# The opening of a Fourier transform and feed-forward kernel: stores, w1 conversions and loads put into another order

## The chip, the cores and the metric

The kernel runs on one core of a Trainium2 chip. Five engines work side by side, each through its own list of instructions in order, and wait for each other by semaphores: TensorE (PE, matrix products; PEld is its weight load), VectorE (DVE), ScalarE (ACT), GpSimd (POOL) and SyncE (SP, which here issues only transfers). Sixteen DMA engines move data between the device memory and the on-chip memory; transfers are issued from SP, ACT or POOL. The metric is the device time of the whole kernel in microseconds (us), the median of several executions.

## The reference

For 8 batches of 3136 rows by 256 columns, the real part of a two-dimensional Fourier transform, then a feed-forward layer with a layer norm ahead of it and a residual around it:

```python
def _attn_ref(x):
    X = np.fft.fft(x, axis=1)
    X = np.fft.fft(X, axis=2)
    return X.real.astype(np.float32)

def _moe_ref(x, g_ln, w_ch1, w_ch2):
    mu = np.mean(x, axis=-1, keepdims=True)
    var = np.mean((x - mu) ** 2, axis=-1, keepdims=True)
    xn = (x - mu) / np.sqrt(var + 1e-06) * g_ln
    ch = np.maximum(xn @ w_ch1, 0.0) @ w_ch2
    return (x + ch).astype(np.float32)
```

`x` of the second function is the result of the first. `w_ch1` is 256 x 1024 and `w_ch2` is 1024 x 256; both come in as 64-bit floating-point numbers, which the kernel reads as 64-bit integers and converts to 32-bit numbers itself.

## The kernel before

**How the work is staged.** The transform along the 3136 rows is done in two steps. Step 1 takes a batch in 7 pieces (`load_x(b, i)`, 512 KB each, the last 256 KB): DVE folds a piece (`fold_zw`, L229 and L230; `fold_eo`, L235 and L236, folds further), PE multiplies it with a table (`step1`, L283 or L289 and L291), ACT copies the result to the tile `s1` (L301), and a transfer (`store1`, L305) writes it to `scratch` in the device memory. `ends` (POOL) and `step1_ends` (PE, then ACT L272) fill one column of `s1` that belongs to the pieces, so a store waits for them too. `relayout` (L312) reads `scratch` back in another order into `s2`; it waits until every store of the batch has landed, and until `clear_scratch` (L256) has put zeros into the rows that no piece fills. Step 2 (`step2(m, ...)`, L345) multiplies `s2` with the table `tab_s` and gives chunks of 256 tokens; "h" is ACT's rounded copy (`ckh`, L366), "l" is DVE's remainder (`ckl`, L370), "f" is ACT's full copy (`ck`, L368; `single`, L352).

**Tiles.** A tile s is one chunk of tokens by 128 of the 1024 hidden columns, 8 tiles to a chunk. `moe1_a(s)` is six products on PE into a PSUM tile `ab` (two buffers), then ACT's copy `asb` (L395), then DVE's two halves of `h` (L396, L397). `moe1_b(s)` is ACT's `h_hi` (L404) and DVE's `h_lo` (L405). `moe2(s)` is twelve products on PE (L440). From tile 6 on a loop runs `moe1_b(s-1)`, `moe1_a(s)`, `moe2(s-3)`, with all else hung into it by lists (`add`, `add_late`).

**Weights.** w1 and w2 come in four quarters each, 512 KB per quarter, into the four parts of one tile, `w1p_all` (`load_w1`, L587; `load_w2(n)`, L592, which overwrites w1's quarter n and so waits for its conversion). A conversion is `convert_m` (DVE, L558 and L560), `convert_z` (ACT, L567), `convert_b` (DVE, L572 and L573) and `finish_w1` (DVE, L601) or `finish_w2` (DVE, L633). For w1 a transform follows, in halves k of the 1024 columns: `transform_w1(k, i)` (PE, L611) takes quarter 2k+i, `round_w1(k)` (ACT, L619) makes the high part, `rest_w1(k)` (PE, L624) and `rest_w1_copy(k)` (ACT, L629) the low part. Tiles 0 to 3 need half k=0 only, tiles 4 to 7 half k=1. `split_w2` is a copy on ACT (L577) and a difference on POOL (L578).

**What sets the order.** On PE, ACT, DVE and POOL the program order is the order of execution for the whole kernel; for the opening, the lines before `main.append(True)`, this holds for SP as well. `warm_up(n, zeros)` is n products of zeros into a PSUM tile that nothing reads (L718).

Of the kernel before, what the change touches and what calls it, by code (L numbers as in the profile page):

```python
# [157 lines left out]
def tile_kernel(ctx: ExitStack, tc: tile.TileContext, x, w1, w2, tu, tab, tz, ty, tw, out):  # L158
# [35 lines left out]
    def load_x(b, i):  # L194
        n = 2 * len(held(i))
        in_order(nc.sync.dma_start(xs[:, i, :n], x[b, i, :, :n]))  # L196
# [22 lines left out]
    def fold_zw(b, i, eng):  # L219

        if i > 3 and b == 0:
            t = weights.tile([128, HW], F32, tag="h_hi", name=f"zw{b}_{i}", bufs=4)
        else:
            t = work.tile([128, 2 * 256], F32, tag="zw", name=f"zw{b}_{i}", bufs=3)
        n = len(held(i))
        z, w = (t[:, 256 * h:256 * h + 128 * n].rearrange("p (s d) -> p s d", s=n) for h in range(2))
        zw[b, i] = z, w
        a, c = xs[:, i, 0:n], xs[:, i, n:2 * n]
        eng.tensor_tensor(out=z, in0=a[:, :, 1:129], in1=c[:, :, 255:127:-1], op=ALU.add)  # L229
        eng.tensor_tensor(out=w, in0=a[:, :, 255:127:-1], in1=c[:, :, 1:129], op=ALU.add)  # L230
# [72 lines left out]
    def store1(b, i, eng=nc.sync):  # L303
        s = s1[b][:, 2 * i:2 * i + len(held(i))]
        in_order(eng.dma_start(scratch[b][2 * i:2 * i + len(held(i))].rearrange("s p d -> p s d"),  # L305
                               s.rearrange("p a h d -> p a (h d)")))
# [257 lines left out]
    def convert_z(key, wp):  # L564
        _, e = conv[key][:2] if key in conv else convert_e(key, wp)
        top = wp.bitcast(BF16).rearrange("p (n four) -> p n four", four=4)[:, :, 3]
        nc.scalar.activation(e, top, AF.Prelu, scale=2.0 ** -112, alpha=2.0 ** 32)  # L567
# [16 lines left out]
    def load_w1(n):  # L584
        wp = w1p_all[:, 4 * n:4 * n + 4].rearrange("p a d -> p (a d)").bitcast(I64)
        i, k = n % 2, n // 2
        nc.sync.dma_start(wp, w1[128 * i:128 * i + 128, 512 * k:512 * k + 512])  # L587
        w1p.append(wp)
# [38 lines left out]
    def rest_w1_copy(k):  # L627
        for j in range(2):
            nc.scalar.copy(w1_cols(w1_lo, k, j), psw.pop((k, j)))  # L629
# [91 lines left out]
    with tc.manual_schedule(engines={E.PE, E.Activation, E.DVE, E.Pool}):  # L721
        with tc.manual_schedule(engines={E.SP}):
            nc.vector.memset(one, 1.0)
            for t in (warm, warm_h):
                nc.vector.memset(t, 0.0)
            for n, t in ((2, warm), (1, warm_h)):
                warm_up(n, t)
            nc.scalar.dma_start(tu_s, tu)
            load_x(0, 0)
            nc.scalar.activation(one, one, AF.Sqrt)  # L730
            for i in range(1, 4):
                load_x(0, i)
            load_w1(0)
            for i in (4, 5, 6):
                load_x(0, i)
            load_w1(1)
            nc.sync.dma_start(tw_all, tw)
            nc.sync.dma_start(tz_s, tz)
            load_w1(2)
            load_w1(3)  # L740
            clear_scratch(0, nc.gpsimd, 0, 2)
            nc.gpsimd.memset(zmu, 0.0)
            nc.gpsimd.memset(masked, 0.0)
            ends(0, 0, 6)
            for i in range(3):
                fold_zw(0, i, nc.vector)
                step1(0, i)
            step1_ends(0, 0, 6)
            for i in range(3):
                store1(0, i, nc.gpsimd)  # L750
            fold_zw(0, 3, nc.vector)
            convert_z("w1_0", w1p[0])
            step1(0, 3)
            ends(0, 6, 10)
            ends(0, 10, NS)
            convert_m("w1_0", w1p[0])
            fold_zw(0, 4, nc.vector)
            convert_b("w1_0")
            nc.vector.tensor_scalar_mul(g_s, tu_s[:, 388:390], 2.0 ** -20)
            finish_w1(0)  # L760
            step1(0, 4)
            step1_ends(0, 6, 10)
            store1(0, 3, nc.gpsimd)
            store1(0, 4, nc.gpsimd)
            for i in (5, 6):
                fold_zw(0, i, nc.vector)
                fold_eo(0, i, nc.vector)
            step1(0, 5)
            convert_m("w1_1", w1p[1])
            step1_ends(0, 10, NS)  # L770
            store1(0, 5, nc.scalar)
            convert_z("w1_1", w1p[1])
            convert_b("w1_1")
            finish_w1(1)
            step1(0, 6)
            store1(0, 6, nc.scalar)
            nc.scalar.dma_start(tab_s[:, :, :gb[4]], tab[:, :, :gb[4]])
            load_w2(0, nc.scalar)
            convert_z("w1_2", w1p[2])
            nc.scalar.copy(minus, tw_all[:, 512:])  # L780
            convert_z("w1_3", w1p[3])
            convert_m("w1_2", w1p[2])
            convert_b("w1_2")
            finish_w1(2)
            convert_m("w1_3", w1p[3])
            relayout(0, 0, 2)
            relayout(0, 2, 4)
            load_w2(1)
            clear_scratch(0, nc.sync, 2, 8)
            load_w2(2)  # L790
            relayout(0, 4, 8)
            nc.sync.dma_start(tab_s[:, :, gb[4]:gb[8]], tab[:, :, gb[4]:gb[8]])
            relayout(0, 8, 16)
            transform_w1(0, 0)
            transform_w1(0, 1)
            round_w1(0)
            convert_b("w1_3")
            load_w2(3)
            nc.sync.dma_start(ty_s, ty)
            nc.sync.dma_start(tab_s[:, :, gb[8]:], tab[:, :, gb[8]:])  # L800
            for i in range(NU):
                load_x(1, i)
            clear_scratch(1, nc.sync)
            finish_w1(3)
            transform_w1(1, 0)
            rest_w1(0)
            convert_z("w2_0", w2p[0])
            rest_w1_copy(0)
            transform_w1(1, 1)
            round_w1(1)  # L810
            convert_m("w2_0", w2p[0])
            convert_b("w2_0")
            f0 = finish_w2(0)
            split(t1_hi, t1_lo, tu_s[:, 0:128])
            convert_z("w2_1", w2p[1])
            convert_m("w2_1", w2p[1])
            warm_up(2, warm_h)
            step2(0, "m")
            step2(0, "h")
            step2(0, "l")  # L820
            step2(1, "m")
            step2(1, "h", 0)
            step2(1, "l", 0)
            convert_b("w2_1")
            f = finish_w2(1)
            moe1_a(0, ((1, 0), (0, 0), (0, 1)))
            split_w2(0, f0)
            moe1_a(1, ((1, 0), (0, 0), (0, 1)))
            rest_w1(1)
            moe1_b(0)  # L830
            split_w2(1, f)
            moe1_a(2)
            moe1_b(1)
            moe1_a(3)
            moe1_b(2)
            rest_w1_copy(1)
            convert_z("w2_2", w2p[2])
            convert_m("w2_2", w2p[2])
            step2(0, "f")
            step2(1, "f")  # L840
            step2(1, "hl", 1)
            moe2(0)
            moe1_b(3)
            moe2(1)
            moe1_a(4)
            convert_b("w2_2")
            f = finish_w2(2)
            nc.gpsimd.tensor_scalar(out=neg, in0=ty_s[:, 1, 129:130], scalar1=2.0, scalar2=-1.0,
                                    op0=ALU.mult, op1=ALU.add)
            step2(2, "m")  # L850
            moe1_b(4)
            moe1_a(5)
            split_w2(2, f)
            step2(2, "hf")
            step2(2, "l")
            moe2(2)
            convert_z("w2_3", w2p[3])
            convert_m("w2_3", w2p[3])
            add_late(6, convert_b, "w2_3")
            add_late(6, lambda: w2f.append(finish_w2(3)))  # L860
            late[7].insert(0, (lambda: split_w2(3, w2f.pop()), ()))

        main.append(True)
        lag, last = 3, 8 * NCH
        for s in range(6, last):
            moe1_b(s - 1)
            moe1_a(s)
            for fn, args in late.get(s, ()):
                fn(*args)
            moe2(s - lag)  # L870
            for fn, args in after.get(s, ()):
                fn(*args)
        moe1_b(last - 1)
        inverse_std(LC)
        moe2(last - 3)
        for i, side in ((0, 0), (1, 0), (0, 1), (1, 1)):
            for t in (last - 2, last - 1):
                moe2(t, ((i, side),))
            finish_last(i, side)
# [19 lines left out]
```

## Time and profile before

| | us |
|---|---|
| median of 3 executions | 982.49 (982.42 to 983.33) |
| the profiled execution | 982.3 |
| its span, first to last instruction | 980.5 |
| so outside the span | 1.8 |

In the rows of the timeline the first number is the start in us from the span's start, the second the time to the end of the last instruction of the row, and the bracket tells how long the engine had been idle and who released it. In the chain of waits the two numbers are the start and the length of a piece. In the table by stretches the columns after the stretch are its length, then the busy time and the number of instructions of PE, PEld, DVE, ACT, POOL, then the TensorE clock that was granted (1.00 is full), the mean busy share of the 16 DMA engines, and GB/s.

### The profile page before, as it was taken

What the parts mean: (1) busy time and instruction counts of PE and PEld (TensorE: products, weight loads), DVE (VectorE), ACT (ScalarE), POOL (GpSimd) and SP (SyncE); (2) the same over time, 40 slices, a digit from 0 to 9 for tenths busy, and PEclk for the clock granted to TensorE, in tenths of its full rate; (3) what the DMA queues carried; (4) which work ended last, traced back from release to release, by engine and by line L of the source; (5) the groups of instructions that cost most, each with busy time, mean ns of one, the idle gap of its engine ahead of it and who ended that gap; (6) DMA issues with size and microseconds to landing.
All of it is one profiled execution on the core that took longest, in us unless ns stands there. A gap on an engine that the chain in (4) does not pass through costs nothing.

```text
span 980.5 us, 21931 instructions
## 1 busy us (share of the span) xinstructions
PE 970.1 (99%) x8366; PEld 957.7 (98%) x8366; DVE 811.5 (83%) x2194; ACT 531.8 (54%) x1416; POOL 235.1 (24%) x288
## 2 busy tenths in 40 slices
PE   8999999999999999999999999999999999999998
PEld 5899999999999999999999999999999999999998
DVE  6888878888888888878888897888888788788887
ACT  3655655555555555555555556555555655554553
POOL 2156342223223133311432133222323200000000
PEclk9999999999999999999999999999999999999999
DMA  9834432213221151221422142211311121100101
GB/s 347 328 122 141 137 139 82 71 54 146 88 87 70 50 189 66 76 76 55 167 77 69 63 155 78 98 55 66 114 55 38 50 66 82 44 22 23 44 22 45
DMA packets 40865, 92.06 MB, mean 94 GB/s; under 512 B 3984, under 2 KB 17296, under 8 KB 39736
## 3 DMA queue, kind: packets, MB, share of 16 engines
q1 hardware_dynamic: 39208, 87.72, 25.1%
q8 instruction: 67, 1.10, 0.5%
q10 hardware_dynamic: 1104, 1.52, 0.4%
q0 software_dynamic: 448, 1.41, 0.4%
q14 instruction: 38, 0.31, 0.1%
HBM read 50.53 MB, written 40.11 MB: 92 GB/s over the span
## 4 chain that ended last, share of the span: by engine, by line
PE 93%; DVE 2%; DMA 2%; ACT 1%; SPq 0%; issue 0%; DVEq 0%
PE acc L440 53%; PE ab L390 26%; PE ps L345 5%; PE psy L465 5%; PE ps L297 3%; DMA xs<-x 1%; DVE h_lo L405 1%; DMA w1p_all<-w 1%; DMA scratch<-s 0%; ACT h_hi L404 0%; DVE h L396 0%; DVE h L397 0%; PE bb L390 0%; PE aa L390 0%; SPq L196 0%
## 5 line engine op out<-in xcount | busy, mean ns | idle before, releaser
L440 PE MATMUL acc<-w_hi,h_lo 128*128 128x256 f32 x1568 | 433.7, 277 | 0.2 <-DVE h_lo L405 0.2
L440 PE MATMUL acc<-w_lo,h_hi 128*128 128x256 f32 x1568 | 433.3, 276 | 0.0
L440 PE MATMUL acc<-w_hi,h_hi 128*128 128x256 f32 x1568 | 433.3, 276 | 0.0
L404 ACT ACTIVATE h_hi<-h 128x512 fp32r<-128x512 f32 x392 | 249.8, 637 | 296.6 <-DVE h L397 296.3
L405 DVE SCALAR_TENSOR_TENSOR h_lo<-h,h_hi 128x512 fp32r<-128x512 f32 x392 | 293.5, 749 | 137.7 <-ACT h_hi L404 135.2
L440 PEld LDWEIGHTS acc<-w_hi,h_lo 128*128 128x128 f32 x1568 | 294.3, 188 | 0.7 <-DVE h_lo L405 0.4
L440 PEld LDWEIGHTS acc<-w_lo,h_hi 128*128 128x128 f32 x1568 | 294.6, 188 | 0.0
L440 PEld LDWEIGHTS acc<-w_hi,h_hi 128*128 128x128 f32 x1568 | 294.4, 188 | 0.0
L390 PE MATMUL ab<-ckl,w_hi 128*128 128x256 f32 x768 | 218.6, 285 | 0.6 <-DVE h L397 0.6
L390 PE MATMUL ab<-ckh,w_lo 128*128 128x256 f32 x768 | 213.3, 278 | 1.5 <-ACT ckh L366 1.5
L390 PE MATMUL ab<-ckh,w_hi 128*128 128x256 f32 x768 | 212.8, 277 | 0.0
L249 POOL TENSOR_TENSOR fl<-f,fh 128x512 fp32r<-128x512 f32 (+1 forms) x49 | 60.2, 1229 | 515.6 <-ACT fh L242 493.4
L396 DVE TENSOR_TENSOR h<-asb,ab 128x256 f32<-128x256 f32 x384 | 158.5, 413 | 1.1 <-ACT asb L395 1.0
L397 DVE TENSOR_TENSOR h<-asb,ab 128x256 f32<-128x256 f32 x384 | 158.4, 413 | 0.0
L390 PEld LDWEIGHTS ab<-ckh,w_lo 128*128 128x128 f32 x768 | 144.9, 189 | 1.7 <-ACT ckh L366 1.7
L390 PEld LDWEIGHTS ab<-ckl,w_hi 128*128 128x128 f32 x768 | 144.8, 189 | 1.6 <-issue 0.9
L390 PEld LDWEIGHTS ab<-ckh,w_hi 128*128 128x128 f32 x768 | 144.8, 188 | 0.0
L395 ACT COPY asb<-ab 128x256 f32<-128x256 f32 x384 | 137.9, 359 | 9.9 <-PE ab L390 2.6
L345 PE MATMUL ps<-tab_s,s 104*128 104x98 f32 (+1 forms) x512 | 65.6, 273 | 0.1
L301 ACT COPY s<-ps 128x510 f32<-128x510 f32 (+1 forms) x56 | 31.1, 555 | 59.5 <-PE ps L297 47.7
L345 PEld LDWEIGHTS ps<-tab_s,s 104*128 104x128 f32 x512 | 61.8, 191 | 0.6 <-PE pw L718 0.6
L366 ACT CAST ckh<-ps 128x392 fp32r<-128x392 f32 (+49 forms) x112 | 39.6, 355 | 37.8 <-PE ps L345 37.5
(112 smaller groups left out, 941.0 us busy)
## 6 DMA issues: line engine op xcount, KB each, us to landing
xs<-x SPq DMA_DIRECT2D x48, 512.0 KB, 4.4
out<-o SPq DMA_DIRECT2D x96, 256.0 KB, 2.0
s<-scratch SPq DMA_DIRECT2D x7, 2048.0 KB, 8.1
scratch<-s SPq DMA_DIRECT2D x42, 256.0 KB, 2.3
w1p_all<-w SPq DMA_DIRECT2D x7, 512.0 KB, 9.8
xs<-x SPq DMA_DIRECT2D x8, 256.0 KB, 3.1
scratch<-s POOLq DMA_DIRECT2D x5, 256.0 KB, 6.6
s<-scratch SPq DMA_DIRECT2D x1, 1024.0 KB, 8.2
```

Source lines behind the costliest of these rows:

```text
L249: nc.gpsimd.tensor_tensor(out=lo, in0=f, in1=hi.bitcast(F32), op=ALU.subtract)
L301: nc.scalar.copy(s[:, :, :255], ps.rearrange("p a h d -> p a (h d)")[:, :, :255])
L345: nc.tensor.matmul(ps[:, h, k0 - base:k1 - base], s2[b][:KP, g, 128 * h:128 * h + 128], tab_s[:KP, h, k0:k1], start=(h == 0 and g == 2 * j ...
L366: nc.scalar.copy(hi, src)
L390: nc.tensor.matmul(pt, wt[wi][:, j, fs], ch[xi][:, j, :w], start=(n == 0), stop=(n == 2))
L395: nc.scalar.copy(asb[:, :w], pa)
L396: nc.vector.tensor_tensor(out=h[:, :w], in0=asb[:, :w], in1=pb, op=ALU.add)
L397: nc.vector.tensor_tensor(out=h[:, w:], in0=asb[:, :m], in1=pb[:, :m], op=ALU.subtract)
L404: nc.scalar.activation(h_hi, h, AF.Relu)
L405: nc.vector.scalar_tensor_tensor(out=h_lo, in0=h, scalar=0.0, in1=h_hi.bitcast(F32), op0=ALU.max, op1=ALU.subtract)
L440: nc.tensor.matmul(acc[c, i][:, side], hs[xi][:, h0:h0 + 128], ws[wi][:, f], start=(f == 0 and side == 0 and n == 0), stop=(f == 7 and n = ...
L465: nc.tensor.matmul(ps[:, j, :n], ck[:, j], ty_s[:, j, :n], start=(j == 0), stop=True, skip_group_check=True)
```

## The change

It concerns the opening alone. The core of the diff, in the order of the code:

```diff
-            for i in range(1, 4):
-                load_x(0, i)
+            load_x(0, 1)
             load_w1(0)
-            for i in (4, 5, 6):
+            for i in range(2, NU):
                 load_x(0, i)
             load_w1(1)
             nc.sync.dma_start(tw_all, tw)
             nc.sync.dma_start(tz_s, tz)
-            load_w1(2)
-            load_w1(3)
...
-            for i in range(3):
-                fold_zw(0, i, nc.vector)
-                step1(0, i)
+            fold_zw(0, 0, nc.vector)
+            step1(0, 0)
+            convert_z("w1_0", w1p[0])
+            fold_zw(0, 1, nc.vector)
+            step1(0, 1)
+            convert_m("w1_0", w1p[0])
+            fold_zw(0, 2, nc.vector)
+            step1(0, 2)
             step1_ends(0, 0, 6)
             for i in range(3):
-                store1(0, i, nc.gpsimd)
+                store1(0, i)
+            load_w1(2)
+            convert_b("w1_0")
             fold_zw(0, 3, nc.vector)
...
-            store1(0, 3, nc.gpsimd)
-            store1(0, 4, nc.gpsimd)
-            for i in (5, 6):
-                fold_zw(0, i, nc.vector)
-                fold_eo(0, i, nc.vector)
+            store1(0, 3)
+            store1(0, 4)
+            fold_zw(0, 5, nc.vector)
+            fold_eo(0, 5, nc.vector)
             step1(0, 5)
+            fold_zw(0, 6, nc.vector)
+            step1_ends(0, 10, NS)
+            store1(0, 5)
+            step1(0, 6)
+            store1(0, 6)
+            convert_z("w1_1", w1p[1])
             convert_m("w1_1", w1p[1])
-            step1_ends(0, 10, NS)
-            store1(0, 5, nc.scalar)
-            convert_z("w1_1", w1p[1])
             convert_b("w1_1")
             finish_w1(1)
-            step1(0, 6)
-            store1(0, 6, nc.scalar)
-            nc.scalar.dma_start(tab_s[:, :, :gb[4]], tab[:, :, :gb[4]])
-            load_w2(0, nc.scalar)
+            nc.sync.dma_start(tab_s[:, :, :gb[4]], tab[:, :, :gb[4]])
+            load_w2(0)
+            relayout(0, 0, 2)
+            relayout(0, 2, 4)
+            load_w1(3)
+            load_w2(1)
+            clear_scratch(0, nc.sync, 2, 8)
+            relayout(0, 4, 8)
+            nc.sync.dma_start(tab_s[:, :, gb[4]:gb[8]], tab[:, :, gb[4]:gb[8]])
             convert_z("w1_2", w1p[2])
             nc.scalar.copy(minus, tw_all[:, 512:])
-            convert_z("w1_3", w1p[3])
+            transform_w1(0, 0)
             convert_m("w1_2", w1p[2])
             convert_b("w1_2")
             finish_w1(2)
...
             transform_w1(0, 1)
             round_w1(0)
+            rest_w1(0)
+            transform_w1(1, 0)
+            rest_w1_copy(0)
+            convert_z("w2_0", w2p[0])
+            convert_m("w2_0", w2p[0])
+            convert_b("w2_0")
+            f0 = finish_w2(0)
+            relayout(0, 8, 16)
+            load_w2(2)
+            warm_up(3, warm_h)
+            step2(0, "m")
+            step2(0, "h")
+            step2(0, "l")
+            step2(1, "m")
+            step2(1, "h", 0)
+            step2(1, "l", 0)
+            moe1_a(0, ((1, 0), (0, 0), (0, 1)))
+            convert_z("w1_3", w1p[3])
+            convert_m("w1_3", w1p[3])
             load_w2(3)
...
+            split_w2(0, f0)
+            moe1_a(1, ((1, 0), (0, 0), (0, 1)))
+            convert_b("w1_3")
             finish_w1(3)
             transform_w1(1, 1)
+            moe1_b(0)
             convert_z("w2_1", w2p[1])
             convert_m("w2_1", w2p[1])
+            moe1_a(2)
+            moe1_b(1)
+            round_w1(1)
             convert_b("w2_1")
             f = finish_w2(1)
+            moe1_a(3)
             rest_w1(1)
             split_w2(1, f)
             moe1_b(2)
             rest_w1_copy(1)
             convert_z("w2_2", w2p[2])
...
+            add_late(13, split, t1_hi, t1_lo, tu_s[:, 0:128])
```

In words: the seven stores go out from SP (five came from POOL, two from ACT), between SP's loads; w1's first quarter is loaded third and converted between the folds of pieces 0 to 3; the last piece is multiplied without its second fold; w1's last quarter is loaded behind the first two relayouts and converted and transformed between tiles 0 to 2, w2's second quarter between tiles 1 to 3; w2's third quarter is loaded behind the big relayout (0, 8, 16) where it was loaded ahead of relayout (0, 4, 8); three warm-up products stand ahead of step 2 where two stood; and the split of the table `t1` moves to the thirteenth tile of the loop. From `convert_z("w2_2")` on, all else stands as before.

More of the change, by code (lines that the diff above doesn't have):

```diff
@@ L744, in tile_kernel @@
             ends(0, 0, 6)
-            for i in range(3):
-                fold_zw(0, i, nc.vector)
-                step1(0, i)
+            fold_zw(0, 0, nc.vector)
[6 more added lines that the diff above has]
+            step1(0, 2)
             step1_ends(0, 0, 6)
             for i in range(3):
-                store1(0, i, nc.gpsimd)
+                store1(0, i)
+            load_w1(2)
+            convert_b("w1_0")
             fold_zw(0, 3, nc.vector)
-            convert_z("w1_0", w1p[0])
+            nc.vector.tensor_scalar_mul(g_s, tu_s[:, 388:390], 2.0 ** -20)
+            finish_w1(0)
             step1(0, 3)
@@ L755, in tile_kernel @@
             ends(0, 10, NS)
-            convert_m("w1_0", w1p[0])
             fold_zw(0, 4, nc.vector)
-            convert_b("w1_0")
-            nc.vector.tensor_scalar_mul(g_s, tu_s[:, 388:390], 2.0 ** -20)
-            finish_w1(0)
             step1(0, 4)
             step1_ends(0, 6, 10)
-            store1(0, 3, nc.gpsimd)
-            store1(0, 4, nc.gpsimd)
-            for i in (5, 6):
-                fold_zw(0, i, nc.vector)
-                fold_eo(0, i, nc.vector)
-            step1(0, 5)
+            store1(0, 3)
+            store1(0, 4)
+            fold_zw(0, 5, nc.vector)
+            fold_eo(0, 5, nc.vector)
+            step1(0, 5)
+            fold_zw(0, 6, nc.vector)
[4 more added lines that the diff above has]
+            convert_z("w1_1", w1p[1])
             convert_m("w1_1", w1p[1])
-            step1_ends(0, 10, NS)
-            store1(0, 5, nc.scalar)
-            convert_z("w1_1", w1p[1])
             convert_b("w1_1")
             finish_w1(1)
-            step1(0, 6)
-            store1(0, 6, nc.scalar)
-            nc.scalar.dma_start(tab_s[:, :, :gb[4]], tab[:, :, :gb[4]])
-            load_w2(0, nc.scalar)
+            nc.sync.dma_start(tab_s[:, :, :gb[4]], tab[:, :, :gb[4]])
[7 more added lines that the diff above has]
+            nc.sync.dma_start(tab_s[:, :, gb[4]:gb[8]], tab[:, :, gb[4]:gb[8]])
             convert_z("w1_2", w1p[2])
             nc.scalar.copy(minus, tw_all[:, 512:])
-            convert_z("w1_3", w1p[3])
+            transform_w1(0, 0)
             convert_m("w1_2", w1p[2])
@@ L784, in tile_kernel @@
             finish_w1(2)
[L785 to L794, printed above, removed]
             transform_w1(0, 1)
             round_w1(0)
-            convert_b("w1_3")
+            rest_w1(0)
[17 more added lines that the diff above has]
+            convert_m("w1_3", w1p[3])
             load_w2(3)
@@ L803, in tile_kernel @@
             clear_scratch(1, nc.sync)
+            split_w2(0, f0)
+            moe1_a(1, ((1, 0), (0, 0), (0, 1)))
+            convert_b("w1_3")
             finish_w1(3)
[L805 to L808, printed above, removed]
             transform_w1(1, 1)
[L810 to L814, printed above, removed]
+            moe1_b(0)
             convert_z("w2_1", w2p[1])
             convert_m("w2_1", w2p[1])
[L817 to L823, printed above, removed]
+            moe1_a(2)
+            moe1_b(1)
+            round_w1(1)
             convert_b("w2_1")
             f = finish_w2(1)
-            moe1_a(0, ((1, 0), (0, 0), (0, 1)))
-            split_w2(0, f0)
-            moe1_a(1, ((1, 0), (0, 0), (0, 1)))
+            moe1_a(3)
             rest_w1(1)
-            moe1_b(0)
             split_w2(1, f)
-            moe1_a(2)
-            moe1_b(1)
-            moe1_a(3)
             moe1_b(2)
```

## The prediction

> **What bounds the kernel now.** First the page's busy times and the summary of its chain of waits:
>
> ```profile
> PE 970.1 (99%) x8366; PEld 957.7 (98%) x8366; DVE 811.5 (83%) x2194; ACT 531.8 (54%) x1416; POOL 235.1 (24%) x288
> ...
> PE 93%; DVE 2%; DMA 2%; ACT 1%; SPq 0%; issue 0%; DVEq 0%
> ```
>
> PE is busy nearly always, and the chain is 93% PE: once the loop runs, PE's own work sets the time, and what the opening can give or take is the moment from which PE is no longer held up. So I read the chain of waits of the first 60 us, piece by piece:
>
> ```profile
> 19.94 4.14 DMA scratch<-s
> ...
> 25.20 5.93 DMA w1p_all<-w
> ...
> 31.15 0.67 ACT ew L567
> ...
> 32.41 3.14 PE ab L390 x12
> ...
> 35.57 0.37 ACT asb L395
> ...
> 36.48 0.52 ACT w_hi L577
> ...
> 38.83 0.96 ACT w_lo L629 x2
> 39.79 0.57 ACT ew L567
> ...
> 41.52 0.54 ACT h_hi L404
> ...
> 42.09 0.69 DVE h_lo L405
> 42.78 0.33 DVE h L396
> 43.11 0.33 DVE h L397
> ...
> 58.96 0.94 PE ab L390 x6
> ```
>
> The last store lands at 24.08; the relayouts may go; ACT then waits for w2's second quarter until 31.13 (`ew L567`), and only behind that conversion copies the first chunk. Tile 0 starts at 32.41. That 32.41 is not what reaches the end, though. At 39.79 stands the conversion of w2's third quarter (`ew L567` again), from there ACT is back to back to `h_hi` of tile 3, DVE takes over at 42.09, and PE takes the chain back only at 58.96 and keeps it. So **the opening is worth exactly as much as the 39.79 moves**: everything from that instruction on stands in the same order in both kernels, on all engines.
>
> Two more facts, from the table by stretches (length, PE, PEld, DVE, ACT, POOL busy, clock, DMA share, GB/s):
>
> ```profile
> 3.00:22.00 19.00, 16.64 (x64) 11.19 (x63) 12.20 (x31) 5.63 (x14) 5.18 (x10) 1.00 1.02 383
> ```
> ```profile
> 30.90:32.40 1.50, 0.01 (x1) 0.00 (x0) 1.21 (x3) 1.20 (x3) 0.00 (x0) 1.00 0.49 190
> 33.00:35.40 2.40, 2.40 (x12) 2.37 (x12) 1.87 (x5) 0.89 (x2) 0.13 (x1) 0.50 0.72 184
> 36.00:40.00 4.00, 4.00 (x32) 3.70 (x32) 3.92 (x9) 3.98 (x9) 1.97 (x2) 1.00 0.98 384
> ```
>
> The transfers are at their limit for the first 22 us (share 1.02, 383 GB/s). And PE, idle for 1.50 us before tile 0, then ran at clock 0.50: its first twelve products took 3.14 us, where six take 0.94 with their tail.
>
> **The change part by part.** I call T' the new start of tile 0 and sum T', then the way from T' to the conversion of w2's third quarter, Z'.
>
> *Stores in SP's queue.* Five issues leave POOL, two leave ACT; neither is on the chain there, so this is worth only what the order of bytes is worth. With all 16 DMA engines busy, the last store lands when the bytes ahead of it are through. w1's last quarter (0.52 MB) no longer stands ahead, nor does what had overtaken it of the first table part and w2's first quarter: 1.4 us for the quarter at 383 GB/s, a little for the rest. I take 22.4 for 24.08 (bounds 21.5 and 23.2). The first store waits for the copies of pieces 0 to 2; POOL's timeline has that wait:
>
> ```profile
> 11.89 2.19 POOL L305 DMA_DIRECT2D scratch<-s  x3 [3.22 <-ACT s L272]
> ```
>
> The third piece is now loaded behind a quarter of w1, so I put the end of this wait at 12.7 instead of 11.89. Now it is SP that waits, with the stores, a quarter of w1 and all else behind it. Five loads issued ahead are then still out (two pieces, a quarter, two tables: 1.66 MB by their shapes, 4.3 us at 383 GB/s), so the DMA engines don't run dry and I cost the wait at nothing; without that cover each us of it would be a us of the last store. The Trainium skill (DMA: Bandwidth & Descriptors, "Issuing engines are not separate DMA queues") says that transfers from all issuers interleave on the same 16 engines and that spreading them only saves issue time. By that rule gathering them on SP earns nothing but order, as summed here; if the queues added up instead, the last store would land later than 24.08, not earlier, and 1.7 us of T' would be gone.
>
> *Relayouts.* In the DMA view the first two landed 3.0 and 4.3 us after their issues at 24.16 and 24.55:
>
> ```profile
> 24.16 0.33 SPq L312
> ...
> 24.55 0.49 SPq L312
> ```
> ```profile
> s<-scratch SPq DMA_DIRECT2D x1, 256.0 KB, 3.0
> ```
> ```profile
> s<-scratch SPq DMA_DIRECT2D x1, 256.0 KB, 4.3
> ```
>
> From 22.4 that makes 25.5 and 27.1: the second product group of step 2 can start at 27.1.
>
> *The PE leg.* The timelines of DVE, PE and ACT:
>
> ```profile
> 20.34 0.75 DVE L601 SCALAR_TENSOR_TENSOR gw<-fw,g_s,ew 128x512 f32<-128x512 f32 x1
> ```
> ```profile
> 23.80 1.98 PE L611 MATMUL psw<-gw,tw_all 128*128 128x512 f32 x4 [0.67 <-DVE gw L601]
> 25.22 1.03 PE L624 MATMUL psw<-w_hi,minus 128*128 128x512 f32 x2
> ...
> 28.00 0.59 PE L718 MATMUL pw<-warm_h 128*128 128x512 bf16 x2
> 28.66 0.69 PE L345 MATMUL ps<-tab_s,s 104*128 104x99 f32 x4
> ...
> 29.36 1.54 PE L345 MATMUL ps<-tab_s,s 104*128 104x98 f32 x12
> ```
> ```profile
> 24.02 1.06 ACT L619 CAST w_hi<-psw 128x512 fp32r<-128x512 f32 x2
> ```
>
> ```profile
> 16.73 1.10 PE L283 MATMUL ps<-f,tu_s 128*128 128x256 f32 x4 [1.42 <-DVE f L236]
> ```
>
> w1's second quarter was ready at 21.09 (20.34 + 0.75), and before that PE had waited 1.42 us for a fold, since w1's first quarter stood ahead of it on DVE. This quarter now goes into DVE's waits for loads, the second fold of the last piece is gone, and ACT's conversion of the second quarter needs only the last copy: I take 20.2 (bounds 19.7 and 21.1). Then one transform (1.98), the rounding that the rest waits for (half of 1.06 beside the transform, half behind it), the rest, to 23.3; the next transform to 25.3; three warm-up products to 26.0; step 2, 2.24 us as before (28.66 to 30.90), to 28.2; the short copy of its second part, 0.3, and a hand-over. **T' = 28.6**, 3.8 us earlier than 32.41, and the two legs (27.1 + 1.1 + 0.4 by the relayout) say the same. Bounds 27.6 and 29.5. The old start's wait for w2's second quarter is really gone.
>
> *From T' to Z'.* Here the moved conversions stand in the way. w1's last quarter in the DVE timeline before:
>
> ```profile
> 23.66 0.42 DVE L558 TENSOR_SCALAR mw<-w1p_all 128x512 int32<-128x512 int32 x1
> 24.12 0.69 DVE L560 SCALAR_TENSOR_TENSOR fw<-w1p_all,mw 128x512 f32<-128x512 uint32 x1
> 24.73 0.29 DVE L572 TENSOR_SCALAR ew<-ew 128x512 int16<-128x512 int16 x1
> 25.05 0.29 DVE L573 TENSOR_SCALAR ew<-ew 128x512 uint16<-128x512 uint16 x1
> 25.38 0.75 DVE L601 SCALAR_TENSOR_TENSOR gw<-fw,g_s,ew 128x512 f32<-128x512 f32 x1
> ```
>
> 23.66 to 24.73 is 1.07 for the first part, 24.73 to 26.13 is 1.40 for the second. DVE is to do: tile 0's `h` (at T' + 0.94 for the products + 0.37 for `asb`; 0.66), the first part (1.07), tile 1's `h` (0.66), the second part (1.40; the two halves of `h` are 0.33 each). So the transform's input is ready at T' + 5.1. (The quarter itself has the place in the queue that w2's second quarter had, which landed at 31.13, 7.0 behind the first relayout's issue: now 29.4, and ACT and DVE want it at T' + 1.3 and T' + 2.0. This cover is half a us; each us later costs one.) **PE has the transform of this quarter in its list ahead of tile 2**, and is through with tile 1 at about T' + 1.5. It stands idle for 3.6 us, with all later tiles queued behind. Then the transform, 1.98, to 7.1; tile 2's products, 0.94, to 8.0; on ACT `asb` (0.37), `h_hi` of tile 1 (0.54), the rounding of half 1 (1.06), `asb` of tile 3: 10.4. Meanwhile DVE does tile 2's `h`, `h_lo` of tile 1 and the second part of w2's second quarter (about 1.35), which ends at 11.05; ACT's split waits for it (0.52), then `h_hi` of tile 2 (0.54) and the rest copy (0.96): **Z' = T' + 13.1 = 41.7**. Before, the same way took 7.4 us (32.41 to 39.79), half clock included. So 3.8 us are won and 5.7 given back: +1.9.
>
> *The clock.* After 1.50 us of idleness PE got half the clock for some 3.4 us and lost 1.7 us. An idle stretch of 3.6 us should bring it down again, beneath the transform and tile 2, which are on the way to Z'. How much falls on work depends on when the drop comes: from 0 (all within the idle time, or no drop) to 1.7 (as before), and more if it lasts twice as long. I take 1.3, nearer to the row. The Trainium skill (TensorE: Matmul & The Clock Gate, "What's actually happening") has half rate after an idle window of about 3.4 us, free-running. The trace dropped after 1.50 us, so measurement and page differ there; 3.6 us lies beyond both. Sum: **+3.2 us**.
>
> *The third quarter's own landing.* It is now issued behind relayout (0, 8, 16), where w2's last quarter stood:
>
> ```profile
> 33.92 0.38 SPq L592 DMA_DIRECT2D w1p_all<-w  x1
> ```
> ```profile
> w1p_all<-w SPq DMA_DIRECT2D x1, 512.0 KB, 8.8
> ```
>
> That quarter landed at 42.7 (33.92 + 8.8). The clearing of `scratch`, for which the queue stops, has the same bytes ahead of it as before; with one 0.52 MB quarter fewer in sum, w2's third lands between 41.3 and 42.7. So even if all else went well, Z' isn't below 41.3, +1.5. At Z' = 43.0 it is hidden.
>
> *At nothing:* the split of `t1`, two short operations on ACT and DVE, goes to the loop, where DVE is busy 83% and PE has the chain; uncovered it would cost what two such instructions cost, under 0.7. The loads behind w2's third quarter come up to a us later and have several to spare.
>
> Sum: 982.3 (span 980.5 + 1.8) + 3.2 = **985.5**; the profiled execution lies 0.2 below the median of 982.49. Less than 2 us, 0.2%, can't be told from no change.
>
> **The rivals.** (1) *The clock holds*, or the drop falls into the idle time: Z' is 41.7, or the landing up to 42.7: 984.2 to 985.2, say 984.7. For it: the 1.42 us ahead of 16.73 brought no drop (clock 1.00 from 3 to 22 us); against it: more than twice that is idle here. Chance 0.22. (2) *The legs are shorter*: T' at 27.5 and a landing near 41.3, or a conversion that fits between: 983.0, the change gives back what it wins. Chance 0.18. (3) *Faster*: the early start is kept. That needs w1's last quarter ready before tile 1's products end, at T' + 1.5, so that PE never waits; then 3.8 us stay won, 978.5. It decides the other way as soon as DVE has tile 0's `h` ahead of the first part, which is its order. Chance 0.07. (4) *The low clock lasts twice as long*, or the queue behind the clearing comes later still: 987.3. Chance 0.08.
>
> **How the numbers follow.** Forecast 985.5, chance 0.45, its own range 984.6 to 986.4. Faster by over 0.2% is rival 3 and a sliver of 2: 0.08. Within 0.2% is most of 2 and the low end of 1: 0.20. Slower: 0.72. The range leaves out rival 3, the lower half of 2 and the top of 4: 983.0 to 987.3.
>
> **What would show it.** Right: tile 0's first product near 28.6; no ACT wait for w2's second quarter ahead of it; a PE idle stretch of 3 to 4 us ahead of L611 behind tile 1, released by DVE's L601; a clock near 0.5 behind it; L567 of w2's third quarter at 42 to 43.5, and PE back in the chain near 62. Wrong: the last store landing behind 23.2; T' below 27; PE going on to tile 2 without that gap; or L567 at or before 39.8, with which the sum turns.

## The result, and the profile after

| | before | after |
|---|---|---|
| median, side by side | 982.45 us (982.13 to 983.33, 4 executions) | 989.34 us (989.07 to 989.68, 4 executions) |
| the profiled execution | 982.3 | 989.07 |
| its span | 980.5 | 987.2 |

The ratio is 1.0068, with an interval of 1.0056 to 1.008: slower by 6.9 us, in the direction of the forecast (+3.2) and above its range, which ended at 987.3. The busy times and the summary of the chain of waits, after:

```profile
span 987.2 us, 21938 instructions
...
PE 973.7 (99%) x8373; PEld 959.3 (97%) x8373; DVE 812.4 (82%) x2192; ACT 532.4 (54%) x1416; POOL 233.0 (24%) x283
...
PE 90%; DVE 6%; DMA 2%; ACT 2%; issue 0%; SPq 0%; ACTq 0%; DVEq 0%
```

PE's share of the chain fell from 93% to 90%, DVE's rose from 2% to 6%. The chain of waits of after, piece by piece (start, length), shows where:

```profile
19.38 4.96 DMA scratch<-s
24.86 4.06 DMA s<-scratch
28.96 1.15 PE ps L345 x8
30.45 1.56 PE ab L390 x6
...
35.90 0.76 DVE gw L601
36.70 3.78 PE psw L611 x4
40.48 0.94 PE ab L390 x6
...
44.55 0.62 ACT w_hi L577
45.18 0.53 ACT h_hi L404
45.71 0.96 ACT w_lo L629 x2
46.67 0.57 ACT ew L567
...
48.42 0.54 ACT h_hi L404
48.98 0.69 DVE h_lo L405
...
85.93 0.93 PE ab L390 x6
```

Tile 0 starts at 30.45 where it started at 32.41: 1.96 us earlier. The conversion of w2's third quarter, the instruction behind which both kernels do the same, stands at 46.67 where it stood at 39.79: 6.88 us later, and the medians lie 6.89 apart. So the way between the two, which took 7.38 us, takes 16.22. PE's own row of that stretch (the timeline; the bracket is the idle time before and who ended it):

```profile
36.70 3.78 PE L611 MATMUL psw<-gw,tw_all 128*128 128x512 f32 x4 [3.43 <-DVE gw L601]
```

The gap that the prediction spoke of is there: PE stands for 3.43 us behind tile 1 until the conversion of w1's last quarter is done. But the transform then takes 3.78, where the same four products took 1.98 before, and tile 0's six took 1.56 ahead of the gap. The table by stretches of after:

```profile
27.20:30.60 3.40, 2.61 (x19) 2.31 (x20) 2.65 (x7) 1.08 (x3) 0.00 (x0) 1.00 0.95 267
30.60:40.90 10.30, 6.87 (x19) 4.50 (x20) 5.85 (x13) 2.81 (x6) 1.81 (x1) 0.50 0.67 227
41.00:42.00 1.00, 1.00 (x10) 0.89 (x8) 0.09 (x1) 0.50 (x2) 0.00 (x0) 1.00 0.88 350
```

The clock is at 0.50 for some 10.3 us, three times the 3.4 us of before, and it fell already under tile 0, ahead of the gap, behind a stretch in which PE was busy for 2.61 of 3.40 us.

### The profile page after: what moved, and what is told of

The parts are those of the page before. It is cut to its first block, busy times and chain, and to the rows that moved or that the text cites. A ratio compares the mean times of both kernels' runs of the same rounds, so it can differ in the third digit from the quotient of the medians.

```text
span 987.2 us, 21938 instructions
## 1 busy us (share of the span) xinstructions
PE 973.7 (99%) x8373; PEld 959.3 (97%) x8373; DVE 812.4 (82%) x2192; ACT 532.4 (54%) x1416; POOL 233.0 (24%) x283
## 4 chain that ended last, share of the span: by engine, by line
PE 90%; DVE 6%; DMA 2%; ACT 2%; issue 0%; SPq 0%; ACTq 0%; DVEq 0%
PE acc L440 50%; PE ab L390 25%; PE ps L345 5%; PE psy L465 4%; PE ps L297 3%; DVE h_lo L405 2%; DVE h L396 1%; DVE h L397 1%; DMA xs<-x 1%; ACT h_hi L404 1%; DMA scratch<-s 1%; DMA s<-scratch 0%; PE psw L611 0%; PE ps L289 0%; DVE st L487 0%
## 5 line engine op out<-in xcount | busy, mean ns | idle before, releaser
L301 ACT COPY s<-ps 128x510 f32<-128x510 f32 (+1 forms) x56 | 31.1, 556 | 59.1 <-PE ps L297 47.4
```

The lines of the kernel that those rows point to most:

```text
L301: nc.scalar.copy(s[:, :, :255], ps.rearrange("p a h d -> p a (h d)")[:, :, :255])
```

## The experiments

The shifts given are (ratio − 1) x 982.5 us, against runs of before on the same chip; after itself is +6.7 by that measure. T' is the start of tile 0 and Z' the conversion of w2's third quarter, each from the profiled execution of the run; before has 32.41 and 39.79, after 30.45 and 46.67.

### PE kept free of the late transform, and the clock kept up

`e1_pe_free` puts the transform and rounding of w1's last quarter behind tile 3's products, so that tiles 2 and 3 needn't wait for it.

```diff
 finish_w1(3)
-transform_w1(1, 1)
...
-round_w1(1)
...
 moe1_a(3)
+transform_w1(1, 1)
+round_w1(1)
 rest_w1(1)
```

> The changed kernel with the transform of w1's last quarter (and its rounding) put behind tile 3's products on PE, so that PE no longer stands 3.4 us ahead of tile 2. Theory S (the order of the moved conversions makes the way from tile 0 to the conversion of w2's third quarter long): that conversion moves from 46.67 to about 44.2, where w2's third quarter lands, and the time falls by 2 to 2.5 us, to 987. Rival C (the low clock is what costs): PE works on through the gap, so the clock may come back one window earlier; 1 us at most, 988. If the opening is decided elsewhere: 989.3, unchanged.

`e2_keep_clock` leaves the order and fills the gap: fourteen products of zeros into a PSUM tile that nothing reads.

```diff
 finish_w1(3)
+keep(14)
 transform_w1(1, 1)
```

> The changed kernel with 14 products of zeros (about 3 us at full clock) on PE in the gap ahead of the transform of w1's last quarter; nothing else is moved. Theory C: the clock comes back at the first window's end, near 34, the transform takes 2.0 us instead of 3.8 and tile 2 0.9: 1.8 to 2.2 us less, 987.2. Theory S without the clock: the gap is still there and only becomes filled, 989.3. If the zeros count as idleness: 989.3 or, where they run past the gap at half clock (6 us for 3.4 us), up to 2 us more.

`e3_pe_free_w2early` is e1 with w2's third quarter loaded ahead of relayout (0, 4, 8), where it was before.

```diff
+convert_m("w1_2", w1p[2])
+load_w2(2)
 relayout(0, 4, 8)
...
-load_w2(2)
 warm_up(3, warm_h)
```

> As e1, and w2's third quarter is issued ahead of relayout (0, 4, 8), as in the kernel before. If in e1 the landing of that quarter (44.2) holds the chain, this one falls further, by 1 to 1.5 us below e1, to 985.7. If e1 is held by ACT and DVE alone, it equals e1 within 0.3 us.

Measured: e1 986.13 (ratio 1.0034, 1.0023 to 1.0045), 3.3 us less than after; e2 987.03 (1.0046, 1.0031 to 1.0061), 2.2 less; e3 984.89 (1.0026, 1.0015 to 1.0038), which can't be told from e1. The chain of waits of e2:

```profile
30.09 1.08 PE ab L390 x6
...
35.87 1.98 PE psw L611 x4
37.85 0.72 PE ab L390 x6
...
43.83 0.68 ACT ew L567
```
```profile
30.60:40.90 10.30, 8.48 (x42) 5.04 (x42) 7.56 (x17) 5.07 (x11) 1.59 (x1) 1.00 0.67 236
```

With the clock at full (the row by stretches, over the time in which after had 0.50), the same order takes 13.74 us from T' to Z' (43.83 − 30.09) in place of 16.22: the price of the order is close to the 13.1 of the prediction, and the clock costs 2.5, not 1.3. Not all of the 2.5 is the zeros' doing. In this execution the clock was up under tile 0 already, ahead of the zeros (1.08 for its six products in place of 1.56, 0.5 us); the transform (1.98 for 3.78) and tile 2 (0.72 for 0.94) make the other 2.0. In e1 the other rows answer, the chain of waits first:

```profile
29.98 1.08 PE ab L390 x6
...
32.62 1.82 DVE fw L560
35.66 0.76 DVE gw L601
36.47 3.65 PE psw L611 x4
...
42.82 0.57 ACT ew L567
```

Z' stands at 42.82, 3.85 us earlier than in after. PE no longer stands behind tile 1 for 3.4 us, but the clock still fell, under the transform (3.65), which here stands behind tiles 2 and 3. And a new thing is on the chain: `fw L560` took 1.82 us where it takes 0.69. The timeline of POOL in e1 has the reason:

```profile
32.60 1.28 POOL L578 TENSOR_TENSOR w_lo<-fw,w_hi 128x512 fp32r<-128x512 f32 x1 [17.37 <-ACT w_hi L577]
```

POOL's instruction began 0.02 us ahead of DVE's, and DVE's ended 0.56 after it (32.62 + 1.82 = 34.44; 32.60 + 1.28 = 33.88), about its usual length. In after, DVE's `ew L572` takes 0.70 in place of 0.29 beside the same instruction of POOL, and ends 0.15 behind it:

```profile
34.83 0.70 DVE L572 TENSOR_SCALAR ew<-ew 128x512 int16<-128x512 int16 x1
```
```profile
33.57 1.81 POOL L578 TENSOR_TENSOR w_lo<-fw,w_hi 128x512 fp32r<-128x512 f32 x1 [17.98 <-ACT w_hi L577]
```

The Trainium skill (SBUF — State Buffer, "SBUF: two separate sides") has GpSimd and VectorE, the latter in a two-port mode or with two inputs from SBUF, share a pair of ports that the one which starts first holds for its whole instruction; these rows agree, with 1.13 us lost in e1 and 0.41 in after.

### Who issues the stores

`e4_stores_back` gives the stores back to POOL and ACT, with the table and w2's first quarter left on SP.

```diff
-    store1(0, i)
+    store1(0, i, nc.gpsimd)
...
-store1(0, 5)
+store1(0, 5, nc.scalar)
...
-store1(0, 6)
+store1(0, 6, nc.scalar)
```

> The changed kernel with the stores issued as before, five from POOL and two from ACT, at the changed places. Theory Q (stores in SP's queue land late, 24.35 where I had 22.4): the last store lands at 22.5 to 23.5, tile 0 starts 1 to 1.8 us earlier than 30.45, and the time falls by as much, to 987.5 to 988.3. If only the order of bytes counts, as I had predicted: the stores land at 24.3 again, 989.3 within 0.5.

`e5_issue_back` also issues the table's first part and w2's first quarter from ACT, behind the last store, as before.

```diff
-nc.sync.dma_start(tab_s[:, :, :gb[4]], tab[:, :, :gb[4]])
-load_w2(0)
...
 store1(0, 6, nc.scalar)
+nc.scalar.dma_start(tab_s[:, :, :gb[4]], tab[:, :, :gb[4]])
+load_w2(0, nc.scalar)
 convert_z("w1_1", w1p[1])
```

> The changed kernel with the stores on POOL and ACT and also the first table part and w2's first quarter on ACT behind the last store, all as before. e4 showed that the stores alone, moved back, land no earlier (24.58), but there SP, no longer held by the stores, issued the table and w2's quarter ahead of them (12.57 and 14.62). Theory Q2 (two causes that hid each other: SP's stores move at about 310 to 330 GB/s from 18 to 22 us, where e4 has 400; and what is issued ahead counts): last store at 22.7 to 23.3, tile 0 near 29.2, 1 us below the changed kernel, 988.3. Rival (the last store is late for its own chain, the last product and copy at 19): 24.3 again, 989.3.

`e8_sp_stores_only` is before with nothing but its seven stores moved to SP.

```diff
-    store1(0, i, nc.gpsimd)
+    store1(0, i)
...
-store1(0, 5, nc.scalar)
+store1(0, 5)
```

> The kernel before with the seven stores issued from SP, behind all of w1's loads, and nothing else. Theory Q2 (stores on SP's queue cost more transfer time than on POOL's): the last store lands 0.5 to 1 us behind 24.08, the time rises by up to as much, 982.5 to 983.4. If the queue is of no account: 982.5 within 0.3.

`e9_pool_all` is after with all seven stores, the table and w2's first quarter issued from POOL, in after's order.

```diff
-    store1(0, i)
+    store1(0, i, nc.gpsimd)
...
-nc.sync.dma_start(tab_s[:, :, :gb[4]], tab[:, :, :gb[4]])
-load_w2(0)
+nc.gpsimd.dma_start(tab_s[:, :, :gb[4]], tab[:, :, :gb[4]])
+load_w2(0, nc.gpsimd)
```

> The changed kernel with all seven stores, the first table part and w2's first quarter issued from POOL, in the changed order; ACT issues none. In e5 the relayouts could go at 22.5, as the prediction had it, but four issues on ACT held up the conversion of w1's second quarter by 2 us and PE came late. Here nothing is added to ACT. Theory Q2 (SP's queue, not the order of bytes, made the last store 2 us late): relayouts at 22.4 to 23, tile 0 at 28.6 to 29.2, the way from there unchanged at 16.2: 987.3 to 988 (less if the clock falls otherwise). Rival (the last store is late for another reason): 989.3.

| | median | ratio, interval | last store lands | T' | Z' |
|---|---|---|---|---|---|
| e4 | 989.95 | 1.0075 (1.006 to 1.009) | 24.58 | 30.63 | 46.88 |
| e5 | 991.99 | 1.0097 (1.0082 to 1.0113) | 22.4 | 31.68 | 48.15 |
| e8 | 985.47 | 1.0031 (1.0018 to 1.0043) | 26.2 | 35.07 | 42.69 |
| e9 | 990.11 | 1.0077 (1.0064 to 1.009) | 22.29 | 31.11 | 46.85 |

None of e4, e5 and e9 gained on after, and e5 lost 2.8 us. In e4, SP, free of the stores, put w1's third quarter on its way at 10.01, the table at 12.57, both ahead of every store, and w2's first quarter at 14.62, ahead of the last four: the order of the bytes was given up with the wait. In e5 the relayouts went out at 22.52, as I had wanted, but the issues held ACT; its timeline:

```profile
19.66 0.98 ACTq L774 DMA_DIRECT2D tab_s<-tab  x1
20.73 0.56 ACTq L592 DMA_DIRECT2D w1p_all<-w  x1
21.34 1.21 ACT L567 ACTIVATE ew<-w1p_all 128x512 bf16<-128x512 bf16 x2 [2.10 <-issue]
```

The conversion of w1's second quarter began at 21.34 where after has it at 19.25, and the whole PE leg came 2 us later with it.

In e9 ACT is free and the last store lands at 22.29, the prediction's 22.4. But more than the issuer differs from after: SP, which no longer stands before the first store, puts w1's third quarter on its way five us earlier (SP's timeline; after first, then e9):

```profile
15.09 1.06 SPq L587 DMA_DIRECT2D w1p_all<-w  x1
```
```profile
10.10 0.33 SPq L587 DMA_DIRECT2D w1p_all<-w  x1
```

e9's relayouts, in the DMA view (size, us from issue to landing), issued from 22.43 on, and under them the two of after, issued from 24.48 on:

```profile
s<-scratch SPq DMA_DIRECT2D x2, 256.0 KB, 5.8
```
```profile
s<-scratch SPq DMA_DIRECT2D x2, 256.0 KB, 3.5
```

Issued two us earlier, they took two us longer. The chains agree: `24.86 4.06 DMA s<-scratch` in after ends at 28.92, and in e9 the same piece ends at 29.36:

```profile
22.82 6.54 DMA s<-scratch
29.41 1.37 PE ps L345 x8
```

e8 shows that the place on SP has a price of its own: 3 us for the stores alone, on the kernel before, where I had put the wait of the queue at nothing. Its SP waits (engine and line, who was waited for, us in all, times, longest):

```profile
SPq L305 <- DMA tab_s<-tab: 4.5, 1, 4.5
SPq L305 <- DMA w1p_all<-w: 2.8, 3, 1.5
```

A store's issue on SP stood still until other transfers had landed, the longest time for a table that ACT had issued, as the profile infers the releasers. The row of the last store's issue fits:

```profile
24.43 0.33 SPq L305 DMA_DIRECT2D scratch<-s  x1
```

ACT issued the table at 18.58, it took 5.8 us to land, and the store, issued at 24.43, landed 1.7 us later: what was lost here is the wait ahead of the issue. The relayouts went out at 26.30 (before 24.16), w2's second quarter behind them, and T' followed.

After and e9 issue the last store at about the same time, 19.38 and 19.46 (DMA view: size, us from issue to landing; after first, then e9):

```profile
scratch<-s SPq DMA_DIRECT2D x1, 128.0 KB, 5.0
```
```profile
scratch<-s POOLq DMA_DIRECT2D x1, 128.0 KB, 2.8
```

The table by stretches has the rates while the stores run, again after and then e9:

```profile
16.00:20.00 4.00, 4.00 (x24) 3.12 (x23) 1.39 (x5) 2.30 (x7) 0.00 (x0) 1.00 1.04 342
```
```profile
16.00:20.00 4.00, 4.00 (x24) 2.95 (x22) 1.31 (x3) 2.61 (x8) 3.88 (x8) 1.00 1.01 387
```

At the same full share, 342 GB/s against 387. The packets differ too (the page's list of DMA queues; before, whose stores left from POOL and ACT, then after):

```profile
q1 hardware_dynamic: 39208, 87.72, 25.1%
...
q0 software_dynamic: 448, 1.41, 0.4%
```
```profile
q1 hardware_dynamic: 41528, 90.35, 25.8%
...
q0 software_dynamic: 48, 0.10, 0.0%
```

1.31 MB left POOL's queue with 400 packets, 3.3 KB each; SP's grew by 2.63 MB and 2320 packets, 1.1 KB each. Of these, 1.32 MB and 960 packets are what ACT's queue (q10) lost, so POOL's 1.31 MB became 1360 packets, 1.0 KB each. The 45 GB/s make 0.18 MB in those 4 us, half a us of the 2.2. No run divides the 2.2 between the issuer with its smaller packets and w1's third quarter: in after it landed at 21.9 (15.09 + 6.8), among the last stores, in e9 at 18.1 (10.10 + 8.0), ahead of them. So the issuer alone isn't shown as the cause. The Trainium skill (DMA: Bandwidth & Descriptors, "Issuing engines are not separate DMA queues") says that spreading over issuers saves only the usually small time of issuing; in e8, where the stores waited on SP to be issued, the issuer was worth 3 us of the whole, which isn't small, so measurement and page differ.

### The order of the conversions

`e6_z_behind` is before with one edit: w2's second quarter is converted behind step 2's last product group rather than ahead of the copies of the first chunk.

```diff
-convert_z("w2_1", w2p[1])
-convert_m("w2_1", w2p[1])
 warm_up(2, warm_h)
...
 step2(1, "l", 0)
+convert_z("w2_1", w2p[1])
+convert_m("w2_1", w2p[1])
```

> The kernel before, with ACT's and DVE's first conversion of w2's second quarter put behind the copies of step 2's chunk (one place later in the code), nothing else. It removes the wait of tile 0 for that quarter's landing (31.13) that the change had removed, without the rest of the change. Theory S: tile 0 starts at 31.3 for 32.41, DVE gets to tile 0's h 0.7 earlier, the conversion of w2's third quarter comes 0.7 to 1.5 us earlier (more if the clock holds): 981 to 981.8. Rival (that wait was hidden, DVE's conversions are the bound): 982.5.

`e7_w1_early` is after with w1's last quarter loaded behind the third, converted there and transformed ahead of step 2.

```diff
 load_w1(2)
+load_w1(3)
...
 transform_w1(1, 0)
+transform_w1(1, 1)
...
-convert_b("w1_3")
-finish_w1(3)
-transform_w1(1, 1)
 moe1_b(0)
```

> The changed kernel with w1's last quarter loaded right behind its third, converted behind it and transformed ahead of step 2, as before; all else changed. Theory S: tile 0 starts later by that quarter's bytes, 1.4 us, at 31.8; the way from there to the conversion of w2's third quarter shrinks from 16.2 to 9 or 10 us; that conversion at 41 to 42, total 983.5 to 984.7. If the moved conversion isn't the cause of the long way, tile 0's later start only adds: 990.5.

`e10_before_best` is e6 with the transform of w1's last quarter behind tile 1, its rounding behind tile 0's `h_hi`, and the rest behind tile 3.

```diff
-transform_w1(1, 1)
-round_w1(1)
...
 moe1_a(1, ((1, 0), (0, 0), (0, 1)))
+transform_w1(1, 1)
 moe1_b(0)
+round_w1(1)
```

> e6 (the kernel before, with one conversion a place later), and the transform of w1's last quarter, which is converted early there, behind tile 1's products on PE, with its rounding behind tile 0's h_hi. PE then reaches step 2 some 2 us earlier and waits for the second relayout (28.85): tile 0 at 30.3 for 31.3. If the way from there stays at 7.2 to 7.7 us: 980.8 to 981.3. Rival (the 2 us on PE and 1 us on ACT only move onto the way): 981.8, as e6, or worse.

`e11_w1_early_w2early` is e7 with w2's third quarter loaded ahead of relayout (0, 4, 8), the edit of e3; `e12_w1_early_w2early_pool` is e11 with the issues of e9.

> e7 with w2's third quarter issued ahead of relayout (0, 4, 8). In e7 ACT waited for that quarter's landing at 42.2. If the landing is the bound there: its conversion at 41.2 to 41.5, 1 us below e7, 985.2 against e7's 986.2 (the profiled one: 983.8 against 984.8). If ACT and DVE are the bound: equal to e7.

> e11 with the issues of e9: the three causes taken out of the changed kernel together (stores on SP's queue, w1's last quarter between the tiles, w2's third quarter behind the big relayout); what is left of the change is the order at the front, w2's second conversion between the tiles and the third warm-up product. If the causes are complete: tile 0 1.5 us earlier than in e11, 983 to 984. If something else of the change costs: 985 or more.

| | median | ratio, interval | T' | Z' |
|---|---|---|---|---|
| e6 | 981.79 | 0.9994 (0.9985 to 1.0003) | 31.34 | 38.55 |
| e7 | 986.17 | 1.0036 (1.0023 to 1.0049) | 32.13 | 42.21 |
| e10 | 982.8 | 1.0006 (0.9997 to 1.0016) | 30.89 | 39.70 |
| e11 | 984.65 | 1.0023 (1.0014 to 1.0032) | 32.73 | 42.36 |
| e12 | 983.39 | 1.0007 (0.9998 to 1.0016) | 31.50 | 41.14 |

e6 takes T' 1.07 earlier with no load or store moved: its tile 0 comes straight behind step 2, and PE has no 1.50 us gap, so the clock stays at 1.00. That brings Z' 1.24 forward in its profile, but the profiled time fell by 0.2 only (982.08 for 982.3); its interval reaches 1, so it can't be told from before. With w1's last quarter early (e7) the gap and the low clock are both gone, but Z' is held by something else, the next piece in e7's chain:

```profile
34.78 7.41 DMA w1p_all<-w
```

That is w2's third quarter, landing at 42.19; ACT stood for it for 0.45 us. The prediction had said that this landing would bound Z' from below, at 41.3 to 42.7, if all else went well; in after it came at 44.1 (35.80 + 8.3), later than that, but was hidden, as forecast. e11 loads it earlier, and what holds Z' then is T' itself (32.73), since the relayouts go out at 25.91 and land at 31.2, behind w1's last quarter. Its Z' is no earlier than e7's: the profiled executions lie up to 1.4 us from the medians (e7's at 984.78, e11's at 985.59), so T' and Z' compare the two no finer than that, and by the intervals e7 and e11 can't be told apart. e12 takes the issues off SP as well; the relayouts go out at 23.74:

```profile
31.50 1.07 PE ab L390 x6
...
41.14 0.56 ACT ew L567
```

The same edit of issuers that gained nothing in e9 gains 1.6 us by the ratios here. The second relayout lands at 28.9 where e11's landed at 31.2, and T' comes 1.23 earlier; in e9 it had landed no earlier than in after. Here, too, more than the issuer changed: w1's third and last quarters leave SP from 10.15 on in e12 and from 14.80 on in e11. By the ratios, of after's 6.7 us the early transform and the early load together take away 4.4 (e11 is at +2.3), the issuers 1.6 more, and 0.7 is left, which can't be told from no change.

e10, which takes an early T' (30.89) and frees tiles 2 and 3 on the kernel before, gained nothing over e6: its clock was at half from 31.1 to 34.5, and Z' is 39.70.

## Why the prediction fell short

**What bounds the kernel: right.** The opening was worth what the 39.79 moved, 6.88 us, to within 0.1 of the medians. PE comes back into the chain only at 85.93 and not near 62. The stretch between, in the table by stretches, has it busy for 37.9 of 39.3 us, and the span grew by 6.7, no more than Z':

```profile
46.67:85.93 39.26, 37.93 (x318) 36.88 (x318) 35.12 (x88) 22.61 (x65) 21.77 (x26) 1.00 0.42 155
```

The prediction's "exactly" isn't shown for a Z' that comes earlier: e6's came 1.24 earlier, and its profiled time fell by 0.2.

**The wait for w2's second quarter: right.** It is gone from the chain, and e6 has its worth: 1.07 us of T', which in the whole time can't be told from nothing.

**The way from T' to Z', 13.1 us without the clock: right in mechanism, 0.6 to 0.7 us too short.** PE's stand of 3.6 us was 3.43, released by `gw L601`. e2 measured 13.74, after without its clock loss 13.8 (16.22, less 0.62 at tile 0 and 1.80 at the transform). 0.41 of the rest is DVE beside POOL, a row that before doesn't show.

**The clock, "I take 1.3": mis-sized, 2.4 measured.** That is the 0.62 and 1.80 just named; e2's rows make it 2.5, and its ratio gets 2.2 back. I had one period of 3.4 us in mind, started by the gap and part of it under the idle time. It was three such periods, and it began before the gap: rival 4 had it lasting longer, but nothing in the prediction had it beginning under tile 0. The gap seems to have prolonged it: in e3, where PE goes on to tiles 2 and 3, the clock fell as early, at 30.0, and was back at 33.4.

**T' = 28.6: the step that failed,** by 1.85 us, half of the miss of 3.7. Its sentence was "From 22.4 that makes 25.5 and 27.1". What failed in after is the 22.4: the last store landed at 24.34, while the 3.0 and 4.3 us from issue to landing came out at 3.0 and 4.1. I costed SP's queue at the rate that the stores had on POOL and ACT, and its wait at nothing. With the issues on POOL the store did land at 22.29 (e9), but there w1's third quarter also left at 10.10 and not at 15.09, so whether the issuer or that wait made the difference stays open. The prediction had named this end, a store behind 24.08 and 1.7 us of T' gone, and none of its rivals carries it. A store at 22.4 wouldn't have been enough either, since the 3.0 and 4.3 us are no constants. e9 issued two us earlier and the second relayout landed at 29.36, against 28.92 in after and 28.85 in before (24.55 + 4.3). While the table, w2's first quarter and w1's last shared the engines, the earlier issue only took longer there. The PE leg was late as well: ready for step 2 at 27.1 (the warm-up's end, 26.28 + 0.81) where I had 26.0, though it wasn't the leg that ended last:

```profile
26.28 0.81 PE L718 MATMUL pw<-warm_h 128*128 128x512 bf16 x3
27.57 0.66 PE L345 MATMUL ps<-tab_s,s 104*128 104x99 f32 x4 [0.48 <-DMA s<-scratch]
```

**"I cost the wait at nothing": wrong.** It held in after in that the DMA engines never ran dry up to the last store (share 1.01), but e8 puts the stores' place on SP at 3 us on the kernel before. In after that cost is covered: taking SP's part away alone (e4, e9) gave nothing, since T' hung on the relayouts' landing, which came no earlier, and Z' on the transform.

The sum of the misses is T' 1.85, the order 0.7 and the clock 1.1: 3.65 of the 3.7.

**Open:** why the second relayout lands near 29 in before, after, e5 and e9 alike, whatever its issue (24.55, 24.86, 22.9 and 22.82); the traces show that it shares the engines, not which of its neighbours would have to go. And what brought the clock down under tile 0 in after, where e1 and e2, with the same opening up to there, kept 1.00. Their T' were 0.4 us earlier and step 2 didn't wait for the second relayout; where it waited (after, e3, e4, e9 and e10) the clock fell, but in e11, with a wait of 0.17, it held. No run varied that alone.

## What to carry to other kernels

A product put into PE's list ahead of a tile makes every later tile wait for its input: before moving a conversion between tiles, work out when its input is ready, and count the clock's fall on top of the gap, for more than one period. A transfer's landing isn't its issue plus a constant while the DMA engines are full: ask what shares them, and whether an earlier issue would only take longer. A transfer's place in the code isn't its place in time: what stands behind a waiting issue in the same list waits with it. An edit that gains nothing in one order may gain in another, so it is tried again behind the other edits (e9 and e12).

## What the hardware showed that I had not expected

The granted clock fell to 0.50 behind a stretch in which PE was busy for 2.61 of 3.40 us with no gap over 0.48 in it, and stayed there for 10.3 us, with a gap of 3.43 in them; in before it fell behind 1.50 us of idleness and stayed for 3.4; with 14 products of zeros in the gap (e2, where it hadn't fallen under tile 0) it held. The Trainium skill (TensorE: Matmul & The Clock Gate, "What's actually happening") ties the fall to an idle window of about 3.4 us; neither fall here had one ahead of it. One instruction of DVE took 1.82 us for 0.69 beside one of POOL. And the last store took 5.0 us to land from SP where it took 2.8 from POOL, issued at about the same time, with w1's third quarter still on its way in the first case and landed in the second.
